# Polysketch attention then RWKV channel mix on one core: merged stores on two queues, another FFN unit order, part of the k features on GpSimd, early loads in turns, split fold

## The chip, the cores and the metric

One core of one Trainium2 chip. The metric is the device time of one execution in microseconds (us), the median of three runs; lower is better.

## What is computed

The reference, cut to what matters (B, H, S, D = 4, 4, 1088, 32; r = 8; d_model = 128; d_ff = 1024; inputs and output float32):

```python
def phi(x):                                   # r*r = 64 features per token and head
    a = einsum('rd,bhsd->bhsr', S1, x); b = einsum('rd,bhsd->bhsr', S2, x)
    return einsum('bhsi,bhsj->bhsij', a, b).reshape(..., r * r)
q_p, k_p = phi(q), phi(k)
kv = einsum('bhsf,bhsd->bhfd', k_p, v); z = sum(k_p, axis=2)
attn = einsum('bhsf,bhfd->bhsd', q_p, kv) / (einsum('bhsf,bhf->bhs', q_p, z)[..., None] + 1e-06)
x = attn as [B, S, H*D]; x_prev = x shifted by one token
xk = mu_k * x + (1 - mu_k) * x_prev;  xr = mu_r * x + (1 - mu_r) * x_prev
out = sigmoid(xr @ w_r) * (relu(xk @ w_k) ** 2 @ w_v)
```

## The kernel before

All input is loaded once, all work is on chip, and one output is stored. The program is a long list of small tasks in the string `ORDER`; each task runs on the engine named behind its slash, and every engine works through its own tasks in that order. A semaphore holds an instruction until what it reads is there, and everything behind it on that engine waits with it.

- **k side, for each batch b.** `KT` transposes k (VectorE), `KP` projects it onto S1 and S2 (TensorE, L344), `KE` copies the result out of PSUM, `KF` forms the 64 products per token and head (`outer`, L327, VectorE; the first factor is read from PSUM), `KA` accumulates them against v in PSUM (L373, L379). Then comes the fold: `KZ` masks the z part (L387), `KC` copies the kv part, `KD` does three matmuls (L398, L400), `KB` and `KW` copy the results into `kvS` and into the weights `SW` of the q side. `KC` waits for `KZ`, and `KD` for both.
- **q side, ten groups g of 128-token tiles.** `QT` transposes q, `Q1` projects (L456), `QE`, `QP`, `QD`, `QI`, `QN` make the denominator and divide, `QF` forms the products (L327), `QR` transposes them on TensorE, `QV` copies them out, `QX` multiplies by kv (L521), `XP`, `XB`, `XK`, `XL`, `XF`, `XE` build the mixed inputs.
- **FFN, ten groups of 1 to 4 tiles (`FS`).** `M1` (L562) multiplies by one 128-column unit of w_k, eight units per group; `RE` is the relu (ScalarE or VectorE), `SQ` the square of two units (mostly GpSimd, L579), `M2` (L591) the second product, `RR` and `SG` the gate, `FN` (L616) the product with the gate.
- **Stores.** `fin` stores a group straight after `FN`: for each of the four 32-row blocks of a 128-token tile one DMA, and one more where a batch ends inside the group. All go out on SyncE's queue (SP, L626), 52 in all.
- **Loads.** SP issues them in one row at the start: k0, S2, v0 in two pieces, q0, w_r, then k, v and q of the other batches. GpSimd (POOL) waits for k0 in a small copy (`gate`, L221) and then issues w_k and w_v (L222, L223), which are cast to bf16. w_k lands as `wkn`, and the task `WKP` (L281, on ScalarE) rewrites it unit by unit into `wk`, so that unit c holds the columns f with f mod 8 = c, as w_v's layout wants it.
- **Dummies.** `dummy` (L248) issues matmuls on zeros: three at the start, one more at `Z/1` in `ORDER`, between the first projection and the first `KA`.

Of the kernel before, what the change touches and what calls it, by code (L numbers as in the profile page):

```python
# [33 lines left out]
QV1_1/ACT KF1_1_0/DVE KA1_0_0/PE/b3 QX1/PE/b4 QD2/DVE KA1_1_0/PE QT1_1/DVE XP1/ACT XB1/ACT XB0/ACT XP0/ACT KZ1/DVE
QI2/DVE RR1/PE/b0 XL0/DVE KC1/ACT QT1_0/DVE XF0/POOL KD1/PE/b3 SG1/ACT XK1/DVE KT2_1/DVE RR0/PE/b0 KW1/ACT KB1/ACT
SG0/ACT Q13/PE/b4 XK0/DVE KT2_0/DVE M10_4/PE/b7 M10_2/PE/b0 M10_5/PE/b3 M10_3/PE/b1 M10_6/PE/b5 QE3/ACT M10_1/PE/b6
RE0_4/DVE RE0_2/ACT RE0_3/ACT QP3/DVE RE0_6/ACT M11_6/PE/b7 RE0_5/DVE M11_0/PE/b0 RE0_1/ACT SQ0_1/POOL M11_1/PE/b1
QD3/DVE M10_7/PE/b5 RE1_6/ACT KP2_0/PE/b3 QN2/DVE RE0_7/ACT QI3/DVE RE1_0/ACT SQ0_2/POOL QF2_1/DVE M10_0/PE/b7
M11_3/PE/b6 RE1_1/ACT KP2_1/PE/b5 RE1_3/ACT QN3/DVE SQ0_3/POOL RE0_0/ACT QF2_0/DVE M11_4/PE/b1 SQ1_0/ACT M11_7/PE/b6
M11_2/PE/b0 Q14/PE/b7 SQ0_0/POOL QF3_1/DVE RE1_4/ACT RE1_2/ACT QR2_0/PE/b1 KE2_0/ACT QT2_0/DVE SQ1_1/ACT QF3_0/DVE  # L40
M20_0/PE/b0 M20_1/PE M20_2/PE QV2_0/ACT M20_3/PE QR2_1/PE/b2 KF2_0_0/DVE RE1_7/ACT QR3_0/PE/b4 KE2_1/ACT QV2_1/ACT
QR3_1/PE/b6 FN0/DVE QV3_0/ACT KF2_1_0/DVE KA2_0_0/PE/b3 QV3_1/ACT QY2/PE/b4 M21_0/PE/b2 M21_1/PE SQ1_3/ACT M11_5/PE/b0
QX3/PE/b6 KT3_0/DVE RE1_5/ACT SQ1_2/ACT QT2_1/DVE KA2_1_0/PE XP2/ACT KT3_1/DVE M21_2/PE XL1/ACT XB2/ACT M21_3/PE
XF1/POOL KP3_0/PE/b0 XP3/ACT XK2/DVE RR2/PE/b5 FN1/DVE XB3/ACT KP3_1/PE/b1 XE0/POOL KZ2/DVE KE3_0/DVE SG2/ACT
M12_4/PE/b2 KC2/DVE M12_0/PE/b4 KE3_1/DVE M12_1/PE/b3 RE2_4/ACT M12_5/PE/b5 KF3_0_0/DVE RE2_1/ACT M12_3/PE/b2
RE2_0/ACT M12_2/PE/b3 RE2_3/DVE RE2_5/ACT M12_7/PE/b0 SQ2_0/POOL M12_6/PE/b4 RE2_2/ACT KF3_1_0/DVE RR3/PE/b2 RE2_6/ACT
KD2/PE/b5 SQ2_1/ACT KA3_0_0/PE/b4 QT3_1/DVE KA3_1_0/PE KB2/ACT KW2/ACT SQ2_2/ACT QT3_0/DVE Q15/PE/b5 XK3/DVE SG3/ACT
M22_0/PE/b1 KZ3/DVE QE5/DVE RE2_7/ACT M13_0/PE/b6 QE4/DVE M13_5/PE/b2 QP5/DVE KC3/ACT QP4/DVE M13_2/PE/b3 RE3_0/ACT
# [63 lines left out]
def kernel(  # L112
# [74 lines left out]
    for b in range(1, B):  # L187
        load_k(b, nc.sync)
        load_v(b, nc.sync)
        load_q(b, nc.sync)  # L190
# [555 lines left out]
```

## Time and profile before

| what | value |
|---|---|
| median of 3 runs | 98.9 us (98.3 to 99.4) |
| the profiled execution's own time | 98.65 us |
| its span in the profile | 96.7 us |

The span is what the profile's times count from; 1.95 us of the profiled time lie outside it. The page gives busy time by engine, the span in forty slices, the DMA queues, and the chain of work that ended last; the views of the trace give single instructions, groups of them, and stretches of time. PE is TensorE's matmuls, PEld its weight loads, DVE VectorE, ACT ScalarE, POOL GpSimd, SP SyncE; a "q" behind an engine's name means its sequencer, which issues DMAs.

### The profile page before, as it was taken

The page shows a single profiled execution, that of the slowest core. Times are in us where ns is not written, and L with a number is a line of the kernel's source. Part 1 is how long each engine was busy: PE and PEld are TensorE (multiplying, and loading weights), DVE is VectorE, ACT ScalarE, POOL GpSimd, SP SyncE. Part 2 cuts the span into 40 slices and gives each one's busy share as a digit, 9 for nine tenths or more (in the row PEclk, how much of TensorE's full clock was granted, in tenths as well). Part 3 has the DMA queues.
Part 4 walks back from the last instruction along what each step waited for, and adds up shares of the span by engine and source line. Part 5 has one row for each costly group of instructions (what it writes and reads, how often), then busy time and mean ns, then how long its engine had stood idle before and what let it go on. Part 6 is the DMA issues. An engine that isn't in the chain of part 4 may idle for free.

```text
span 96.7 us, 3021 instructions
## 1 busy us (share of the span) xinstructions
...
## 2 busy tenths in 40 slices
...
GB/s 79 236 204 258 306 286 297 293 262 350 237 209 21 26 8 27 34 0 0 7 8 101 0 7 0 40 68 53 66 0 0 41 68 63 56 0 66 88 107 41
DMA packets 9278, 9.70 MB, mean 100 GB/s; under 512 B 1456, under 2 KB 7984, under 8 KB 9264
## 3 DMA queue, kind: packets, MB, share of 16 engines
...
q0 software_dynamic: 288, 0.52, 2.9%
q8 instruction: 9, 0.15, 0.6%
q10 hardware_dynamic: 304, 0.00, 0.2%
q14 instruction: 5, 0.04, 0.1%
...
## 4 chain that ended last, share of the span: by engine, by line
PE 50%; DVE 19%; DMA 9%; ACT 5%; SPq 5%; issue 3%; ACTq 0%
PE ps_o L591 12%; PE ps_h L562 10%; DMA hdq<-in_q_dram 8%; PE ps_qtp L500 6%; PE ps_abw L456 6%; PE ps_x L521 4%; PE ps_kab L344 4%; DVE XK L534 4%; PE ps_kv L373 3%; DVE k L572 3%; DVE qp L327 3%; SPq L626 3%; PE ps_r L603 2%; DVE kT L337 1%; DMA out_dram<-osb 1%
## 5 line engine op out<-in xcount | busy, mean ns | idle before, releaser
L579 POOL TENSOR_TENSOR k<-k 128x1024 bf16<-128x1024 bf16 (+1 forms) x20 | 32.5, 1638 | 15.0 <-ACT k L570 13.0
L570 ACT ACTIVATE k<-ps_h 128x512 bf16<-128x512 f32 (+3 forms) x55 | 25.7, 540 | 1.7 <-PE ps_h L562 1.6
L562 PE MATMUL ps_h<-XK,wk 128*128 128x512 bf16 (+3 forms) x74 | 18.8, 344 | 1.0 <-DVE k L572 0.2
L591 PEld LDWEIGHTS <-k 128*128 128x128 bf16 x272 | 16.2, 98 | 4.4 <-issue 2.3
L591 PE MATMUL ps_o<-wv,k 128*128 128x128 bf16 x272 | 18.5, 219 | 0.1
L581 ACT ACTIVATE k<-k 128x1024 bf16<-128x1024 bf16 (+2 forms) x17 | 16.2, 968 | 0.1
L572 DVE TENSOR_SCALAR k<-ps_h 128x512 bf16<-128x512 f32 (+2 forms) x25 | 14.4, 622 | 0.1
L327 DVE TENSOR_TENSOR kp<-ps_kab,ab 128x512 f32<-128x512 f32 (+3 forms) x10 | 10.8, 1112 | 1.6 <-ACT ab L313 1.5
L327 DVE TENSOR_TENSOR qp<-an,ps_abw 128x512 f32<-128x512 f32 x17 | 11.2, 677 | 0.1
L456 PE MATMUL ps_abw<-SW,qT 128*128 128x96 f32 (+1 forms) x72 | 9.8, 280 | 0.6 <-DVE SW L315 0.6
L500 PE MATMUL ps_qtp<-ident,qp 128*128 128x128 f32 x68 | 9.3, 274 | 1.0 <-DVE qp L327 1.0
L562 PEld LDWEIGHTS <-wk 128*128 128x128 bf16 x80 | 7.1, 99 | 4.7 <-issue 1.3
L547 POOL TENSOR_SCALAR PP<-XL,omu_k 128x31 f32<-128x31 f32 x4 | 1.5, 381 | 18.7 <-DVE XL L315 12.5
L456 PEld LDWEIGHTS ps_abw<-SW,qT 128*128 128x128 f32 (+1 forms) x72 | 8.4, 185 | 2.1 <-DVE SW L315 0.8
L500 PEld LDWEIGHTS ps_qtp<-ident,qp 128*128 128x128 f32 x68 | 7.4, 141 | 1.9 <-PE ps_abw L456 1.1
L313 ACT COPY qpT<-ps_qtp 128x512 f32<-128x512 f32 (+1 forms) x14 | 6.7, 523 | 1.0 <-PE ps_qtp L500 0.9
L248 PE MATMUL wt<-zero 128*128 128x512 f32 x8 | 6.4, 952 | 1.1 <-DVE warm L156 1.1
L534 DVE SCALAR_TENSOR_TENSOR XK<-ps_x,mu_k,PP 128x512 bf16<-128x512 f32 (+8 forms) x13 | 6.7, 534 | 0.7 <-ACT XB L313 0.7
L344 PE MATMUL ps_kab<-SW,kT 128*64 128x64 f32 x144 | 6.0, 227 | 1.5 <-ACT qpT L313 1.3
L373 PEld LDWEIGHTS ps_kv<-kp,vt 128*32 128x32 f32 x288 | 4.5, 110 | 3.9 <-issue 1.9
L344 PEld LDWEIGHTS ps_kab<-SW,kT 128*64 128x64 f32 x144 | 4.9, 137 | 2.8 <-ACT qpT L313 1.4
L373 PE MATMUL ps_kv<-kp,vt 128*32 128x64 f32 x288 | 5.5, 221 | 1.3 <-DMA vt<-in_v_dram 0.8
...
## 6 DMA issues: line engine op xcount, KB each, us to landing
...
vt<-in_v_dram SPq DMA_DIRECT2D x4, 256.0 KB, 10.7
...
```

The lines of the kernel that those rows point to most:

```text
L327: nc.vector.tensor_mul(o.rearrange("p t h i j -> p (t h) i j"), _ap(a_, [[sa, y], [1, R], [0, R]]), _ap(b_, [[sb, y], [0, R], [1, R]]))
L344: nc.tensor.matmul(p[64 * c:64 * c + 64, (t - t0) * 64:(t - t0) * 64 + 64], kT[b][:, t, 64 * c:64 * c + 64], SW[:, 0, :H, :2, :], skip_gro ...
L373: nc.tensor.matmul(kv[32 * h:32 * h + 32, :64], vt[b][:, h, T, :], kp[:, t, h].rearrange("p i j -> p (i j)"), start=(T == 0), stop=(T == 8 ...
L456: nc.tensor.matmul(p[lo:hi, t * 96:t * 96 + 96], qT[:, s + lo:s + hi], SW[:, (s + lo) // S, g % 2:g % 2 + H].rearrange("p h x r -> p (h x ...
L500: nc.tensor.transpose(p[:, t * P:t * P + P], qp[g][:, t, 2 * pair:2 * pair + 2].rearrange("p h i j -> p (h i j)"), ident[:])
L534: nc.vector.scalar_tensor_tensor(XK[:, b * S + s:b * S + s + m], tiles[f"x_{g}"][:, c0:c0 + m], mu_k[:], PP[:, b * XW + s:b * XW + s + m], ...
L562: nc.tensor.matmul(h[:, :n * P], wk[:, c], XK[:, F0[g] * P:(F0[g] + n) * P])
L570: nc.scalar.activation(o, i, RELU)
L572: nc.vector.tensor_scalar(o, i, 0.0, None, op0=mybir.AluOpType.max)
L579: (nc.vector if eng == "DVE" else nc.gpsimd).tensor_mul(k2[:, :, :n * P], k1[:, :, :n * P], k1[:, :, :n * P])
L581: nc.scalar.activation(k2[:, :, :n * P], k1[:, :, :n * P], mybir.ActivationFunctionType.Square)
L591: nc.tensor.matmul(o[:, t * P:t * P + P], k2s[g, j][:, c, t * P:t * P + P], wv[:, w * j + c, :], start=(j == 0 and c == 0 and t == 0), sto ...
```

## The change

1. **Stores.** `FN` only computes; the stores are tasks of their own (`OD`), 36 instead of 52. Where four tiles of a group lie in one batch, the form stays (32 rows by 4 tiles by 128, four DMAs). Elsewhere one DMA stores a whole 128-token tile, its DRAM side written as 4 by 32 by 128; the tile that holds a batch's end goes in two of 2 by 32 by 128. 31 go out on SP; the last five (two of group 8, all three of group 9) on ACT.
2. **FFN unit order.** Unit c = 4x + e now holds the columns 512x + 4f + e. The weights are read in place, with a step of four elements between columns (`wkc`), `WKP` and `wkn` are gone, and w_v is loaded in the matching layout.
3. **k features on GpSimd.** The features of every batch are in two pieces per half, and nine of the sixteen run on POOL, which reads both factors from `ab` in SBUF.
4. **Early loads in turns.** q0, w_r and everything behind them are issued after small POOL copies that wait for k0, and k1 and all behind it after one that waits for v0.
5. **Split fold.** `KD` is the z matmul alone and waits for `KZ`; `KG` holds the other two and waits for `KC`; `KC` no longer waits for `KZ`.
6. **Order.** All of `ORDER` is new; `Z/1` is gone.

```diff
 ORDER = """
-Z/1 KA0_0_0/PE/b1 KA0_0_1/PE KF0_1_1/DVE KA0_1_0/PE KA0_1_1/PE QT0_0/DVE KZ0/DVE QT0_1/DVE KC0/ACT WRP/POOL KD0/PE/b1
+KD0/PE/b2 KG0/PE WRP/POOL KW0/ACT Q11/PE/b0 KB0/DVE Q10/PE/b1 QE1/DVE Q12/PE/b2 QP1/DVE QE0/DVE QD1/DVE QP0/DVE
...
-    gate = const.tile([P, 1], F32)
-    nc.gpsimd.tensor_copy(gate[:], hdk[0][:, 0, 0, :1])
-    nc.gpsimd.dma_start(wkn[:], moe_w_k)
-    nc.gpsimd.dma_start(wv[:], moe_w_v.rearrange("(p c) d -> p c d", p=P))
+    nc.gpsimd.tensor_copy(hdq[0][:, 0, :1], hdk[0][:, 0, 0, :1])
+    load_q(0, nc.sync)
+    nc.gpsimd.tensor_copy(wr_f[:, :1], hdk[0][:, 0, 0, :1])
+    nc.sync.dma_start(wr_f[:], moe_w_r)
+    nc.gpsimd.dma_start(wk[:], moe_w_k)
+    nc.gpsimd.dma_start(wv[:].rearrange("p (x e) d -> p x (e d)", e=4), moe_w_v.rearrange("(x p e) d -> p x (e d)", p=P, e=4))
+    nc.gpsimd.tensor_copy(hdk[1][:, 0, 0, :1], vt[0][:, 0, 0, :1])
+    for b in range(1, B):
+        load_k(b, nc.sync)
+        load_v(b, nc.sync)
+        load_q(b, nc.sync)
...
+        if eng == "POOL":
+            a_ = ab[:, 1, t0:t1]
+        outer(kp[:, t0:t1], a_, ab[:, 0, t0:t1], nc.gpsimd if eng == "POOL" else nc.vector)
...
+    wkc = wk[:].rearrange("p (x f e) -> p x e f", e=4, f=P)
...
-        nc.tensor.matmul(h[:, :n * P], wk[:, c], XK[:, F0[g] * P:(F0[g] + n) * P])
+        nc.tensor.matmul(h[:, :n * P], wkc[:, c // 4, c % 4], XK[:, F0[g] * P:(F0[g] + n) * P])
...
+    def stores(g):
+        n, res, t = FS[g], [], 0
+        while t < n:
+            b, x = divmod((F0[g] + t) * 4, NB)
+            m = min(n - t, (NB - x) // 4)
+            if m == 4:
+                res += [(b, x + y, m, 4, 32 * y, 32, t, m) for y in range(4)]
+            elif m:
+                res += [(b, x + 4 * i, 4, 1, 0, P, t + i, 1) for i in range(m)]
+            else:
+                res += [(b, x, 2, 1, 0, 64, t, 1), (b + 1, 0, 2, 1, 64, 64, t, 1)]
+                m = 1
+            t += m
+        return res
+    def store(g, i, eng):
+        b, x, m, step, p0, np_, t, tt = stores(g)[i]
+        o = osb[g][p0:p0 + np_, t:t + tt, :]
+        dst = orow[b][:, x:x + step * (m - 1) + 1:step, :]
+        if tt == 1:
+            o, dst = osb[g][p0:p0 + np_, t, :], dst.rearrange("a y f -> y a f")
+        (nc.scalar if eng == "ACT" else nc.sync).dma_start(dst, o)
```

SP at the end of the program before: the stores from group 6 on, all on this queue (the last 16 are groups 7, 8 and 9).

```order
L626 DMA out_dram<-osb 32x4x128 x4
L626 DMA out_dram<-osb 32x3x128
L626 DMA out_dram<-osb 32x128
L626 DMA out_dram<-osb 32x3x128
L626 DMA out_dram<-osb 32x128
L626 DMA out_dram<-osb 32x2x128 x4
L626 DMA out_dram<-osb 32x4x128 x4
L626 DMA out_dram<-osb 32x3x128 x4
```

SP at the same place now (group 6, then 7, then half of 8):

```order
L652 DMA out_dram<-osb 32x4x128 x4
L652 DMA out_dram<-osb 4x32x128
L652 DMA out_dram<-osb 2x32x128 x2
L652 DMA out_dram<-osb 4x32x128 x2
L652 DMA out_dram<-osb 32x4x128 x2
```

And ACT at the end of its program now, behind its last square and the last gate:

```order
L591 ACTIVATE k_1707<-k_1657 128x2x384
L619 ACTIVATE r<-ps_r 128x384
L652 DMA out_dram<-osb 32x4x128 x2
L652 DMA out_dram<-osb 4x32x128 x3
L770 UNCONDITIONAL_BRANCH
```

Sixteen stores stood on one queue behind `FN` of group 7; now seven stand there and five on ACT, three of them behind the last `FN`.

POOL before, from its first wait on a load to the first `XF` (names with hdk_72, vt_80, hdq_76 are k0, v0, q0):

```order
L221 COPY gate<-hdk_72 128x1
L222 DMA wkn<-in_moe_w_k_dram 128x1024
L223 DMA wv<-in_moe_w_v_dram 128x1024
L224 TENSOR_SCALAR omu_k<-mu_k 128x1
L225 TENSOR_SCALAR omu_r<-mu_r 128x1
L231 TENSOR_SCALAR wr_p<-wr_f,omu_r 128x128
L231 TENSOR_SCALAR wr_c<-wr_f,mu_r 128x128
L547 TENSOR_SCALAR PP<-XL,omu_k 128x31
```

POOL now (hdk_73 is k1):

```order
L217 COPY hdq_76<-hdk_72 128x1
L219 COPY wr_f<-hdk_72 128x1
L221 DMA wk<-in_moe_w_k_dram 128x1024
L222 DMA wv<-in_moe_w_v_dram 128x2x512
L223 COPY hdk_73<-vt_80 128x1
L229 TENSOR_SCALAR omu_k<-mu_k 128x1
L230 TENSOR_SCALAR omu_r<-mu_r 128x1
L324 TENSOR_TENSOR kp<-ab 128x512
L236 TENSOR_SCALAR wr_c<-wr_f,mu_r 128x128
L236 TENSOR_SCALAR wr_p<-wr_f,omu_r 128x128
L324 TENSOR_TENSOR kp<-ab 128x768
```

A piece of batch 0's features (kp<-ab) now stands on POOL behind the copy that waits for v0.

ACT before, from the first copy of the fold to the first copies of the q features:

```order
L313 COPY kvs<-ps_kv 128x64
L313 COPY kvS<-ps_kf 128x128
L281 COPY wk<-wkn 128x128x8
L313 COPY wsb<-ps_abw 128x128
L313 COPY qpT<-ps_qtp 128x256 x2
L313 COPY ab<-ps_kab 128x16x2x8
```

ACT now:

```order
L310 COPY kvs<-ps_kv 128x64
L310 COPY SW<-ps_kf 128x4x8
L310 COPY SW<-ps_kf 128x8
L310 COPY wsb<-ps_abw 128x128
L310 COPY ab<-ps_kab 128x16x2x8
L310 COPY qpT<-ps_qtp 128x256 x2
```

The rewriting of w_k is gone from between the fold and the copies that VectorE and TensorE wait for; `kvS` went to VectorE.

## Rows read from the trace of the kernel before

**Rows 1.** The page: its first line.

```profile
span 96.7 us, 3021 instructions
```

**Rows 2.** Busy time in two stretches: stretch, length, engines' busy us, PEclk, DMA share, GB/s.

```profile
16.00:24.00 8.00, 5.93 (x161) 4.30 (x161) 7.00 (x17) 5.77 (x14) 0.58 (x3) 1.00 1.05 307
...
26.00:88.00 62.00, 59.35 (x864) 44.48 (x869) 58.04 (x129) 55.73 (x119) 36.80 (x37) 1.00 0.18 38
```

**Rows 3.** The same view: the end of the span, and a part of it.

```profile
88.00:96.70 8.70, 0.00 (x0) 0.00 (x0) 0.19 (x1) 0.00 (x0) 0.00 (x0) 0.69 0.38 77
...
92.00:94.00 2.00, 0.00 (x0) 0.00 (x0) 0.00 (x0) 0.00 (x0) 0.00 (x0) 0.50 0.52 107
```

**Rows 4.** The output tensor, from 86.4 us to the end.

```profile
L626 SPq DMA_DIRECT2D out_dram<-osb x16: 315/425/466, 86.6 to 93.9; - x16
...
DMA to landing us min/median/max: 1.5/1.7/1.8
```

**Rows 5.** The chain that ended last, its last compute: start us, us, what.

```profile
85.72 1.88 PE ps_o L591 x32
...
87.63 0.56 DVE osb L616
```

**Rows 6.** DMA queues: packets, MB, share of 16 engines.

```profile
q0 software_dynamic: 288, 0.52, 2.9%
...
q10 hardware_dynamic: 304, 0.00, 0.2%
```

**Rows 7.** Timeline of the start: start us, us, engine, line, operation, idle before and releaser.

```profile
7.57 2.75 DVE L327 TENSOR_TENSOR kp<-ps_kab,ab 128x512 f32<-128x512 f32 x4 [1.22 <-ACT ab L313]
...
9.54 0.43 PE L373 MATMUL ps_kv<-kp,vt 128*32 128x64 f32 x16 [0.79 <-DMA vt<-in_v_dram]
...
11.32 0.21 ACT L313 COPY kvs<-ps_kv 128x64 f32<-128x64 f32 x1 [3.12 <-DVE zm L387]
...
12.95 2.02 PE L456 MATMUL ps_abw<-SW,qT 128*128 128x96 f32 x16 [0.59 <-DVE SW L315]
13.28 4.79 ACT L281 COPY wk<-wkn 128x1024 bf16<-128x1024 bf16 x1 [0.61 <-DMA wkn<-in_moe_w_k_dram]
...
15.72 1.48 DVE L337 STREAM_TRANSPOSE kT<-hdk 128x256 f32<-128x256 f32 x4
...
18.21 0.29 DVE L471 TENSOR_TENSOR pw<-ps_abw,wsb 128x128 f32<-128x128 f32 x1 [0.89 <-ACT wsb L313]
...
18.48 0.80 PE L344 MATMUL ps_kab<-SW,kT 128*64 128x64 f32 x20 [1.26 <-ACT qpT L313]
...
19.01 2.62 DVE L327 TENSOR_TENSOR kp<-ps_kab,ab 128x1024 f32<-128x1024 f32 x2
```

**Rows 8.** The chain again: q0's load, the last `XK` before the FFN, six `M1`.

```profile
3.00 7.69 DMA hdq<-in_q_dram
...
24.84 0.33 DVE XK L534
...
79.75 1.46 PE ps_h L562 x6
```

**Rows 9.** Groups on DVE, shapes apart: line, engine, operation, out<-in, count, busy us, mean ns.

```profile
L327 DVE TENSOR_TENSOR kp<-ps_kab,ab 128x1280 f32<-128x1280 f32 x3 | 4.5, 1485 | 0.3 <-ACT ab L313 0.3
...
L327 DVE TENSOR_TENSOR kp<-ps_kab,ab 128x1024 f32<-128x1024 f32 x3 | 3.7, 1221 | 0.1
...
L327 DVE TENSOR_TENSOR kp<-ps_kab,ab 128x512 f32<-128x512 f32 x3 | 2.0, 685 | 1.2 <-ACT ab L313 1.2
```

**Rows 10.** Groups on POOL, the same columns.

```profile
L579 POOL TENSOR_TENSOR k<-k 128x1024 bf16<-128x1024 bf16 x16 | 30.1, 1894 | 12.2 <-ACT k L570 10.2 <-DVE k L572 1.9
L579 POOL TENSOR_TENSOR k<-k 128x256 bf16<-128x256 bf16 x4 | 2.4, 612 | 2.8 <-ACT k L570 2.8
...
L231 POOL TENSOR_SCALAR wr_p<-wr_f,omu_r 128x128 bf16<-128x128 f32 x1 | 0.6, 610 | 3.2 <-DMA wr_f<-in_moe_w_r_dram 3.2
```

**Rows 11.** Groups on TensorE, the same columns: `M1`'s weight loads.

```profile
L562 PEld LDWEIGHTS <-wk 128*128 128x128 bf16 x80 | 7.1, 99 | 4.7 <-issue 1.3
```

More of the change, by code (lines that the diff above doesn't have):

```diff
@@ L34 @@
[L34 to L48, printed above, removed]
@@ new lines @@
+SQ0_1/ACT QF2_1/DVE M10_4/PE/b7 KA2_0_0/PE/b4 SG1/ACT SQ0_3/POOL RE0_4/ACT QD3/DVE RE1_5/ACT M20_0/PE/b3 QT2_1/DVE
+M20_1/PE RE1_2/ACT QR2_1/PE/b7 SQ0_2/POOL RE1_3/ACT KP2_1/PE/b6 QV2_1/ACT QI3/DVE SQ1_1/POOL QT2_0/DVE M20_2/PE
+M20_3/PE QN3/DVE M11_4/PE/b1 KE2_1/ACT M11_6/PE/b7 M11_0/PE/b5 FN0/DVE QR2_0/PE/b2 RE1_4/ACT QF3_1/DVE OD0_0/DMA
+KF2_1_1/POOL RE1_0/ACT M11_7/PE/b1 RE1_6/ACT Q14/PE/b3 QF3_0/DVE QV2_0/ACT RE1_7/ACT KT3_0/DVE M11_1/PE/b7
+KF2_1_0/POOL QR3_1/PE/b0 RE1_1/ACT QR3_0/PE/b1 QE4/DVE SQ1_0/ACT KT3_1/DVE KP3_0/PE/b2 QY2/PE/b7 QV3_0/ACT M21_0/PE/b5
@@ new lines @@
+QV3_1/DVE SQ1_3/POOL M21_1/PE KE3_0/ACT KA2_1_0/PE QT3_1/DVE QX3/PE/b0 SQ1_2/POOL KC2/ACT KZ2/DVE QT3_0/DVE QP4/DVE
+KD2/PE/b4 QD4/DVE KF3_0_0/POOL XP2/ACT XB2/DVE KG2/PE M21_2/PE XL1/ACT QI4/DVE M21_3/PE XB3/ACT XK2/DVE RR2/PE/b1
+XF1/POOL XP3/ACT KP3_1/PE/b6 QN4/DVE KF3_0_1/POOL FN1/DVE KW2/ACT M12_5/PE/b7 QF4_1/DVE KB2/ACT OD1_1/DMA RR3/PE/b5
+KE3_1/ACT SG2/ACT XK3/DVE Q15/PE/b4 OD1_0/DMA XE0/POOL KF3_1_0/POOL SG3/ACT QF4_0/DVE M12_1/PE/b1 RE2_5/ACT
+M13_3/PE/b0 M13_4/PE/b5 RE2_1/ACT QE5/DVE M13_1/PE/b2 KF3_1_1/DVE QR4_0/PE/b7 RE3_3/ACT M13_6/PE/b1 RE3_4/DVE
@@ L75 @@
+SQ8_2/ACT M27_3/PE RE9_0/DVE M19_1/PE/b3 M19_3/PE/b0 SQ8_3/POOL FN7/DVE M19_2/PE/b7 SQ8_1/ACT M28_0/PE/b5 RE9_2/DVE
+M19_4/PE/b6 OD7_0/DMA M19_6/PE/b4 M19_7/PE/b1 RE9_1/DVE RE9_4/ACT M19_5/PE/b2 OD7_3/DMA M28_1/PE RE9_3/DVE RE9_6/ACT
+OD7_2/DMA M28_2/PE RE9_5/ACT RE9_7/DVE OD7_1/DMA RR9/PE/b0 SQ9_1/ACT SQ9_0/DVE M28_3/PE OD7_4/DMA SQ9_3/DVE SQ9_2/ACT
+M29_0/PE/b1 FN8/DVE M29_1/PE SG9/ACT M29_2/PE OD8_3/ACT OD8_0/DMA M29_3/PE OD8_2/DMA OD8_1/ACT FN9/DVE OD9_1/ACT
+OD9_0/ACT OD9_2/ACT
 """
@@ L184 @@
     load_v(0, nc.sync)
-    load_q(0, nc.sync)
-    nc.sync.dma_start(wr_f[:], moe_w_r)
[L187 to L190, printed above, removed]
     ident = const.tile([P, P], F32)
@@ L276 @@
         add(nm, {"POOL": 0.6, "ACT": act(128, 0.105)}, lambda e, o=o, m=m: wr_mix(o, m, e), ["Lr"])
-    def wk_perm(eng):
-        o, i = wk[:].rearrange("p c f -> p f c"), wkn[:].rearrange("p (f c) -> p f c", c=NC)
-        if eng == "ACT":
-            nc.scalar.copy(o, i)
-        else:
-            nc.gpsimd.tensor_copy(o, i)
-    add("WKP", {"POOL": 2.2, "ACT": act(DFF)}, wk_perm, ["Lw"])
     QS = [2, 2, 4, 4, 4, 4, 4, 4, 4, 2]
```

125 lines of the change are left out of this document (64 added, 61 removed).

## The prediction

> **What bounds the kernel now.** I read the span first [rows 1], then busy time by stretch [rows 2, 3], then the chain of waits where compute ends [rows 5], then the output's DMAs [rows 4], and last the timeline of the start [rows 7]. Three parts show.
>
> The end: the last `FN` finishes at 87.63 + 0.56 = 88.2 us [rows 5], the span at 96.7 [rows 1]. In the 8.5 us between, every engine is empty but for that product [rows 3]. SP meanwhile issues sixteen stores one after the other, the first at 86.6 and the last at 93.9 us, so 7.3 / 15 = 0.49 us apart [rows 4]; the last lands 1.7 us after its issue, at 95.6, and 1.1 us of closing follow it. The queue's issue rate sets the end: compute has long been done.
>
> The middle: from 26 to 88 us PE is busy for 59.4 of 62 us, DVE for 58.0 and ACT for 55.7; POOL for 36.8 [rows 2]. Matmuls overlap in the pipeline, so PE's share is flattered. Nobody owns this stage: DVE and PE lead and wait for each other.
>
> The start, up to the last `XK` that the first FFN matmuls need (24.84 + 0.33 = 25.2 us [rows 8]): k features on DVE, the fold, then a DVE-heavy q stretch (7.0 of 8 us from 16 to 24 [rows 2]). ACT spends 4.79 us on rewriting w_k from 13.28, and behind it DVE waits 0.89 us for a copy and PE 1.26 us [rows 7].
>
> **The end, part by part.** FN9 still closes the compute; call its end T. Then three stores are issued by ACT, which has nothing else left. At SP's spacing of 0.49 the third is issued at T + 0.05 + 0.98. If it lands as before, 1.7 us later, and 1.1 us follow, the span ends at T + 3.8. That is the fast bound.
>
> The slow bound comes from the new form. Before, each store's outer dimension was 32 rows on both sides. Now it is 128 rows in SBUF but 4 in DRAM. The queue rows show what an outer dimension does: on q0 two weight loads of 128 rows each left 288 packets, 256 of data and 2 x 16 others; on q10 the 8-row S1 and the two 128-row mu vectors left 304 packets, 264 of data and 40 others, that is 16 + 16 + 8 [rows 6]. I read one closing packet per DMA engine in use: sixteen for 128 rows, eight for 8. Four outer rows would then mean four engines, each with 32 packets of 512 B where it had 8. From 92 to 94 us the 16 engines were 0.52 busy at 107 GB/s [rows 3]: 209 packets per us for 8.3 engine-us per us, so 40 ns each. A store's 8 packets take 0.32 us of its 1.7. Three new stores on the same four engines need 96 x 0.040 = 3.8 us behind 0.05 + 1.4, and with the 1.1 the span ends at T + 6.4.
>
> I take T + 5.1, halfway: I believe the four engines, but the 40 ns were measured with all sixteen writing, and four alone should be quicker. The tail shrinks from 8.5 to 5.1, **-3.4 us** (bounds -2.1 and -4.7). Other stores cost nothing where they stand: their queue was idle for most of the run, and the five of group 7 are issued while groups 8 and 9 are computed. The price if that cover fails is their own time on two or four engines, inside the slow bound.
>
> The Trainium skill, "DMA: Bandwidth & Descriptors", section "Why a DMA increments its semaphore by 16 and not by 1", says that a transfer runs on the largest number of engines up to 16 that divides the slowest dimension of both sides. The 8 of S1 agrees. By it the new stores use four engines, the half tiles two; the sum would then lean to the slow bound, against this change. No row here shows a four-row transfer.
>
> **The start.** *KF0 on POOL.* DVE loses one 512-column piece: its four took 2.75 us, until 10.3 [rows 7]; three end some 0.69 earlier [rows 9]. But on POOL the piece stands behind the copy that waits for v0, and v0 came at 9.54 [rows 7]. Two small instructions later, near 10.0, the piece starts. No POOL row has this shape. From 256 and 1024 columns bf16 [rows 10], (1894 - 612) / 768 = 1.67 ns a column, 0.18 fixed: 1.04 us. The only wide f32 row, 128 columns in 0.61 [rows 10], gives at most 3.3 ns, 1.9 us. I take 1.2, the same operation being the nearer row, so the piece ends at 11.2, 0.9 after the old end of the features: **+0.7**, since `KA`'s first quarter is done by then.
>
> *Split fold.* Before, from the kv copy (11.32) to the first projection (12.95) passed 1.6 us [rows 7], with mask, copy, fold, `KB` and `KW` in series. Now mask and copy go side by side and `KW` needs the first matmul alone: **-0.3**.
>
> *WKP gone.* The waits of 0.89 on DVE and 1.26 on PE go [rows 7]; they overlap, DVE is the fuller engine: **-0.9**. Late next is DVE itself.
>
> *Features of batch 1.* Of 2.62 us on DVE [rows 7] 768 columns go to POOL: **-0.9**. But `KB`, one `XP` and one `XB` move onto DVE in this stretch, and one `XL` leaves it: **+0.7**.
>
> *Loads in turns.* k0 ends as before and q0's issue slips while v0 still fills the engines, so I leave its landing at 3.00 + 7.69 = 10.7 [rows 8]: 0. `KZ` now stands on DVE behind a q0 transpose of about a microsecond, which then ends just with `KA`, near 11.7; each tenth that q0 is later shows, bounds 0 and +1. k1 now waits until v0 has landed; at some 300 GB/s [rows 2] its 0.56 MB take 1.9 us, and with issue and landing it is there at 13 to 14.5. Its transposes stood at 15.72 without a wait [rows 7] and move up to about 14.4: 0 to +0.8, I take **+0.2**. *Dummy gone:* PE was idle there in any case; PEclk was 1.00 in all compute stretches shown [rows 2]. The bounds are 0 and, if the clock fell to half for the early matmuls, some +2; I take 0.
>
> Sum -0.5; bounds -2 and +3. The FFN starts at 24.7 where it started at 25.2.
>
> **The middle.** Of the features of batches 2 and 3, 2 x (1.485 + 1.221) = 5.4 us of DVE [rows 9], all but one 512-column piece (0.69) go: -4.7. The new order gives DVE other work: two more relus, two more `QE`, `XB` and `XP` on net against ACT, which costs about half of it. Both engines together lose some 4 us, two each. POOL takes seven pieces, 4096 columns: 7 x 0.18 + 4096 x 1.67 ns = 8.1 us, at the wr_p rate 14.8; with 36.8 of 62 it has 25 free [rows 2]. PE has not a microsecond less. As it leads as often as DVE, I let 1.5 of the 2 us show: **-1.5**, bounds 0 and -4.
>
> Strided weights: no row has a step of four elements. 80 loads take 99 ns each beside matmuls [rows 11]; bounds 0, and the rival below. I take 0.
>
> **Sum.** -3.4 - 0.5 - 1.5 = -5.4: span 91.3, and with 1.95 outside it 93.25, against the profiled 98.65. That execution lies 0.25 below the median of the three runs, 98.9; I forecast **93.3**.
>
> **Rivals.**
> *A. The stores keep all sixteen engines.* For it: the same packets and bytes as before; against: the eight closing packets of the 8-row load. Tail T + 3.8: 92.0.
> *B. The middle and the start give nothing: PE holds them.* For it: PE's 59.4 of 62 us, and POOL's late first piece; against: DVE's 58.0 and the matmuls' overlap. Only the tail: 98.65 - 3.4 = 95.3.
> *C. DVE was the bound.* For it: 7.0 of 8 us before 24, 58.0 of 62 after; against: ACT close behind, and PE. Then 4.0 of the 4.7 us show: 93.3 - 2.5 = 90.8.
> *D. Slower: the strided w_k.* A step of four elements reads 8 bytes for 2. If that stretches a load fourfold, 80 loads of 396 ns stand where 99 did. Six `M1` in a row take 1.46 us [rows 8], 0.24 each, so about 0.15 us per load shows: 80 x 0.15 = +12, 105.3. It decides when a load shows by 5.4 / 80 = 68 ns, that is from about 0.31 us on. Against: today's 99 ns hide behind 0.24.
> The Trainium skill, "TensorE: Matmul & The Clock Gate", sections "LDWEIGHTS" and "Weight-path perf modes", lets a load's time follow its column count, and allows steps up to 1,024 elements for the fast load; by this rule D costs nothing. Only contiguous loads are in this trace.
>
> **How the numbers follow.** Forecast 0.47, A 0.2, B 0.18, C 0.11, D 0.04. The range, 90.6 to 95.8, runs from C to B with B's half microsecond of spread; outside it are D, the slow side of B and the fast side of C, under 0.2. About 1% is what a measurement of this kernel can tell from no change: faster 0.94 (all but D and the far side of B), same 0.02, slower 0.04.
>
> **What would show it.** Right: the last compute near 86 us, three ACT issues behind it, 5 us to the span's end; landing of the new stores well over 1.7 us; the last `XK` before the first FFN matmuls near 24.7; no ACT wait of DVE near 18; L562's successor still loading in about 99 ns; POOL near 48 us busy. Wrong: landing at 1.7 (A); compute still ending at 88 (B) or before 84 (C); weight loads far over 99 ns (D); a PEclk under 1.00 before 24 us.

## The result, and the profile after

The changed kernel takes 95.43 us, median of 4 runs (94.91 to 97.02), against 98.9 us: ratio 0.963, 95% interval 0.955 to 0.971. The forecast was 93.3 with 90.6 to 95.8. A ratio here compares the runs near each kernel's fastest, so it can lie below the ratio of the medians; medians and spread are given beside it.

The profiled run took 94.91 us. Its windows (stretch, then busy us of PE, PEld, DVE, ACT and POOL, PEclk, DMA share, GB/s), which answer to [rows 2, 3]:

```profile
8.00:16.00 8.00, 5.65 (x109) 4.99 (x110) 4.88 (x16) 0.66 (x4) 2.71 (x6) 0.73 1.10 262
16.00:24.00 8.00, 7.08 (x133) 5.58 (x136) 7.15 (x21) 2.69 (x8) 1.51 (x1) 0.63 1.05 298
26.00:88.00 62.00, 59.41 (x868) 46.68 (x874) 56.58 (x133) 54.80 (x119) 45.30 (x45) 1.00 0.19 45
88.00:92.90 4.90, 0.00 (x0) 0.00 (x0) 0.00 (x0) 0.00 (x0) 0.00 (x0) 0.72 0.26 75
```

ACT's w_k copy is gone, POOL has 8.5 us more in the middle, and the granted clock, 1.00 from 16 to 24 us before, is 0.63 there and 0.73 in the eight us ahead.

The timeline of its start (start us, us, engine, line, operation, idle before and releaser), which answers to [rows 7]:

```profile
8.35 0.18 POOL L223 COPY hdk<-vt 128x1 f32<-128x1 f32 x1 [2.13 <-DMA vt<-in_v_dram]
8.36 0.43 PE L372 MATMUL ps_kv<-kp,vt 128*32 128x64 f32 x16 [0.67 <-DVE kp L324]
...
8.81 1.06 POOL L324 TENSOR_TENSOR kp<-ab 128x512 f32<-128x512 f32 x1
...
9.93 0.47 PE L372 MATMUL ps_kv<-kp,vt 128*32 128x64 f32 x18 [1.09 <-POOL kp L324]
...
11.12 0.21 ACT L310 COPY kvs<-ps_kv 128x64 f32<-128x64 f32 x1 [2.93 <-PE ps_kv L378]
11.37 0.19 DVE L386 TENSOR_TENSOR zm<-ps_kv,mask 128x32 f32<-128x32 f32 x1 [0.54 <-ACT kvs L310]
...
11.61 0.64 PE L396 MATMUL ps_kf<-zm,S 128*128 128x32 f32 x2 [0.55 <-DVE zm L386]
12.18 0.70 PE L402 MATMUL ps_kf<-ident,kvs 128*64 128x128 f32 x4
12.92 0.25 ACT L310 COPY SW<-ps_kf 128x32 f32<-128x32 f32 x2 [1.59 <-PE ps_kf L402]
...
13.23 3.73 PE L463 MATMUL ps_abw<-SW,qT 128*128 128x96 f32 x16 [0.35 <-ACT SW L310]
...
25.73 0.80 DVE L541 SCALAR_TENSOR_TENSOR XK<-ps_x,mu_k,PP 128x256 bf16<-128x256 f32 x2
```

The sixteen matmuls of q's first projection, 2.02 us before [rows 7], take 3.73; they start 0.28 later than before. The last `XK` ends at 25.73 + 0.80 = 26.53, where it ended at 25.17 [rows 8].

How long this start takes varies with the loads. Two kernels of the tail experiments below have the same program up to here; their last `XK` ends at 27.82 (first line) and 25.63 (second line), after waits for q0 of 1.77 and 0.43 us where the changed kernel's profile has none. In both the granted clock falls as well, to 0.55 and 0.70 from 16 to 24 us.

```profile
27.02 0.80 DVE L541 SCALAR_TENSOR_TENSOR XK<-ps_x,mu_k,PP 128x256 bf16<-128x256 f32 x2
```

```profile
24.83 0.80 DVE L541 SCALAR_TENSOR_TENSOR XK<-ps_x,mu_k,PP 128x256 bf16<-128x256 f32 x2
```

DVE's last three `FN`, the output's DMAs from 83 us (duration ns min/median/max, first and last start us), a window of the tail, and the queues; they answer to [rows 3 to 6]:

```profile
82.31 0.69 DVE L628 TENSOR_TENSOR osb<-ps_o,r 128x512 f32<-128x512 f32 x1 [0.25 <-issue]
85.71 0.69 DVE L628 TENSOR_TENSOR osb<-ps_o,r 128x512 f32<-128x512 f32 x1
87.06 0.56 DVE L628 TENSOR_TENSOR osb<-ps_o,r 128x384 f32<-128x384 f32 x1 [0.66 <-ACT r L619]
...
L652 SPq DMA_DIRECT2D out_dram<-osb x7: 323/542/560, 83.0 to 86.8; - x7
L652 ACTq DMA_DIRECT2D out_dram<-osb x5: 385/547/653, 86.4 to 88.9; - x5
...
90.00:92.00 2.00, 0.00 (x0) 0.00 (x0) 0.00 (x0) 0.00 (x0) 0.00 (x0) 0.54 0.20 60
...
q1 hardware_dynamic: 7484, 8.65, 35.6%
q0 software_dynamic: 416, 0.52, 3.2%
q10 hardware_dynamic: 988, 0.33, 1.4%
```

The last `FN` ends at 87.62, the span at 92.9. So the three parts come to: start +1.36 (25.17 to 26.53), middle -1.93 (63.02 to 61.09 us), tail -3.23 (8.51 to 5.28). Forecast: -0.5, -1.5, -3.4.

### The profile page after: what moved, and what is told of

It is laid out like the page before. It is cut to its first block, busy times and chain, and to the rows that moved or that the text cites. A ratio compares the mean times of both kernels' runs of the same rounds, so it can differ in the third digit from the quotient of the medians.

```text
span 92.9 us, 3009 instructions
## 1 busy us (share of the span) xinstructions
PE 80.3 (86%) x1197; PEld 61.9 (67%) x1203; DVE 73.8 (80%) x186; ACT 63.0 (68%) x145; POOL 54.0 (58%) x75
## 4 chain that ended last, share of the span: by engine, by line
PE 43%; ACT 28%; DVE 8%; DMA 6%; issue 5%; POOL 2%; SPq 2%; DVEq 0%; ACTq 0%; POOLq 0%
ACT k L580 12%; PE ps_abw L463 8%; ACT k L591 7%; PE ps_qtp L507 7%; PE ps_h L572 6%; DMA vt<-in_v_dram 6%; PE ps_kv L372 6%; PE ps_kab L341 4%; PE ps_o L601 3%; PE ps_x L528 3%; ACT qpT L310 3%; ACT r L619 2%; DVE kT L334 2%; PE ps_kf L402 2%; ACT PP L537 2%
## 5 line engine op out<-in xcount | busy, mean ns | idle before, releaser
L589 POOL TENSOR_TENSOR k<-k 128x1024 bf16<-128x1024 bf16 (+2 forms) x21 | 33.1, 1588 | 9.9 <-ACT k L580 7.6
L582 DVE TENSOR_SCALAR k<-ps_h 128x512 bf16<-128x512 f32 (+2 forms) x27 | 15.9, 628 | 1.7 <-PE ps_h L572 1.7
L591 ACT ACTIVATE k<-k 128x1024 bf16<-128x1024 bf16 (+3 forms) x17 | 16.8, 1027 | 0.1
L324 POOL TENSOR_TENSOR kp<-ab 128x512 f32<-128x512 f32 (+1 forms) x9 | 10.9, 1216 | 10.2 <-ACT ab L310 9.6
L463 PE MATMUL ps_abw<-SW,qT 128*128 128x96 f32 (+1 forms) x72 | 11.4, 309 | 0.5 <-ACT SW L310 0.5
L463 PEld LDWEIGHTS ps_abw<-SW,qT 128*128 128x128 f32 (+1 forms) x72 | 10.3, 216 | 1.8 <-ACT SW L310 1.1
L572 PEld LDWEIGHTS <-wk 128*128 128x128 bf16 x80 | 8.0, 115 | 4.0 <-DVE XK L541 0.8
L310 ACT COPY qpT<-ps_qtp 128x512 f32<-128x512 f32 (+1 forms) x15 | 8.0, 545 | 2.5 <-PE ps_qtp L507 2.3
L628 DVE TENSOR_TENSOR osb<-ps_o,r 128x512 f32<-128x512 f32 (+3 forms) x10 | 6.1, 607 | 1.7 <-ACT r L619 0.7
L324 DVE TENSOR_TENSOR kp<-ps_kab,ab 128x512 f32<-128x512 f32 (+1 forms) x7 | 4.9, 726 | 1.8 <-ACT ab L310 1.8
```

The lines of the kernel that those rows point to most:

```text
L310: nc.scalar.copy(o, i)
L324: eng.tensor_mul(o.rearrange("p t h i j -> p (t h) i j"), _ap(a_, [[sa, y], [1, R], [0, R]]), _ap(b_, [[sb, y], [0, R], [1, R]]))
L463: nc.tensor.matmul(p[lo:hi, t * 96:t * 96 + 96], qT[:, s + lo:s + hi], SW[:, (s + lo) // S, g % 2:g % 2 + H].rearrange("p h x r -> p (h x ...
L572: nc.tensor.matmul(h[:, :n * P], wkc[:, c // 4, c % 4], XK[:, F0[g] * P:(F0[g] + n) * P])
L582: nc.vector.tensor_scalar(o, i, 0.0, None, op0=mybir.AluOpType.max)
L589: (nc.vector if eng == "DVE" else nc.gpsimd).tensor_mul(k2[:, :, :n * P], k1[:, :, :n * P], k1[:, :, :n * P])
```

## The experiments

Three questions: why the start became longer, what made the tail shorter, and what gave the middle. Ratios are to the kernel before, run beside each. In the edits to `ORDER`, only the stretch of a line that changed is shown.

### The start: fillers and the GpSimd piece

**The filler put back** (`Z`: two matmuls of 512 columns whose result nobody reads):

```diff
-KA0_0_0/PE/b2 KF0_1_0/DVE
+Z/1 KA0_0_0/PE/b2 KF0_1_0/DVE
```

> The changed kernel with the one block of filler matmuls put back on TensorE between the first projection and the first state matmuls, as the kernel before had it. Theory 1 (clock): without the filler TensorE stood empty from 7.7 to 8.4 us and from 8.8 to 9.9, and its granted clock fell to half from 11.6 to 21.9 us; that is what made the start 1.35 us longer instead of 0.5 shorter. Then PEclk reads 1.00 from 8 to 24 us, the 16 matmuls of the first projection of q (L463) go from 3.73 back to about 2.0 us, the last XK ends near 25.2 instead of 26.5, and the time falls by 1.0 to 1.6 us, to about 94.1. Theory 1b: the clock matters, but the wait for the GpSimd piece (1.09 us) is still there, and one filler is not enough: the fall comes later or is shorter. Theory 2 (rival): the start is held by the GpSimd piece and by the work moved onto VectorE, and a slower TensorE is hidden: the last XK stays at 26.5 +- 0.3 and the time at 95.4 +- 0.4, whatever the clock.

Median 95.88 us, ratio 0.951 (0.946 to 0.957); of the six runs two took 94.2 us, at a mean clock of 0.966, and four 95.6 to 96.6, at 0.93. The profiled run is one of the two. Its clock is 1.00 to 16 us and falls after that; its last `XK` ends at 25.59:

```profile
16.00:24.00 8.00, 6.52 (x158) 5.10 (x158) 6.91 (x20) 3.16 (x10) 2.06 (x4) 0.79 1.06 254
```

In this profile it is theory 1b: the fall comes later and is shorter. By the median (95.88 against 95.43) one filler alone gains nothing.

**Three fillers**:

```diff
-KF0_1_1/DVE KA0_0_1/PE KA0_1_0/PE QT0_1/DVE KA0_1_1/PE
+KF0_1_1/DVE Z/1 KA0_0_1/PE KA0_1_0/PE QT0_1/DVE KA0_1_1/PE Z/1
```

(and the one above).

> The changed kernel with three blocks of filler matmuls: the one of before, one while TensorE waits for the GpSimd piece, one between the state matmuls and the fold. Theory 1: the clock stays at 1.00 to 24 us and the last XK ends at 25.2 or earlier, time 93.8 to 94.4; if one filler is enough, no better than with one, and the third may cost up to 0.5 us where it stands in front of the fold (the wait there was 0.55 us, a block of two matmuls takes about 1.1 us at the full clock where nothing overlaps). Theory 2: 95.4 +- 0.4 or later.

93.98 us, ratio 0.949 (0.945 to 0.952), 1.45 below the changed kernel; five of the six runs lie from 93.65 to 94.13, one at 98.19. Two windows of it, and three rows of its timeline:

```profile
8.00:16.00 8.00, 7.34 (x122) 4.68 (x121) 5.67 (x18) 1.04 (x5) 2.71 (x6) 1.00 1.12 261
16.00:24.00 8.00, 6.49 (x172) 5.00 (x172) 8.00 (x23) 3.50 (x11) 2.34 (x5) 1.00 1.05 297
...
9.21 1.12 PE L253 MATMUL wt<-zero 128*128 128x512 f32 x2
...
13.32 2.02 PE L463 MATMUL ps_abw<-SW,qT 128*128 128x96 f32 x16 [0.35 <-ACT SW L310]
...
23.64 0.80 DVE L541 SCALAR_TENSOR_TENSOR XK<-ps_x,mu_k,PP 128x256 bf16<-128x256 f32 x2
```

The granted clock is 1.00 in both stretches, the projection is back at 2.02 us, and the last `XK` ends at 24.44, 2.1 us earlier. VectorE, which waited for TensorE in the changed kernel (7.15 of 8 us busy from 16 to 24), is now busy for all 8.00. Theory 2 falls for the changed kernel: VectorE doesn't cover a TensorE at half clock. A part is given back: last `XK` to last `FN` is 62.0 us here, 61.1 in the changed kernel.

**The kernel before without its filler**:

```diff
-Z/1 KA0_0_0/PE/b1 KA0_0_1/PE
+KA0_0_0/PE/b1 KA0_0_1/PE
```

> The kernel before without its block of filler matmuls (it computes nothing that is used); nothing else is changed. Theory 1: the loss belongs to the filler alone: the granted clock falls to half at some 11 to 12 us for about ten us, the first projection of q takes about 3.7 instead of 2.02 us, and the time rises by 1 to 2 us, 98.9 to about 100.3. Theory 1b: the filler is not enough by itself, the GpSimd wait of the changed kernel is needed too: the clock stays at 1.00 and the time at 98.9 +- 0.4. Theory 2: the clock may fall, but VectorE covers it: time 98.9 +- 0.5.

99.08 us, ratio 0.999 (0.995 to 1.004). The clock dips late, and nothing follows:

```profile
16.00:24.00 8.00, 6.98 (x160) 5.40 (x160) 6.97 (x17) 5.23 (x14) 0.35 (x2) 0.79 1.06 308
```

Theory 1 in its first form falls: the filler alone was worth nothing to the kernel before. There the dip stayed without effect on the time, as theory 2 had it.

**The first GpSimd piece back on VectorE**, no fillers:

```diff
-KF0_0_1/POOL
+KF0_0_1/DVE
```

> The changed kernel with the one piece of batch 0's k features that went to GpSimd put back on VectorE; the fillers stay out, the later pieces stay on GpSimd. Theory 1b (the clock falls because filler and GpSimd wait come together): without the GpSimd wait TensorE is idle no longer than in the kernel before without its filler, so the clock falls briefly or not at all (0.79 or more in 16 to 24 us), the last XK ends near 25.2, time 94.2 to 94.9. Theory 1 in its first form (the filler alone): the clock falls as in the changed kernel and the time stays at 95.4. Rival of both: the piece costs VectorE its 0.69 us and the start gets longer: last XK at 26.5 or later, time 95.4 to 96.1.

Median 94.67 us, ratio 0.937 (0.930 to 0.944); three runs took 92.7 to 94.0 us (mean clock 0.982 to 0.996) and five 94.6 to 96.1 (0.929 to 0.967). In the profiled run, of 94.0 us, the clock is 1.00 up to 24 us and the last `XK` ends at 25.27:

```profile
16.00:24.00 8.00, 5.36 (x160) 3.97 (x156) 7.07 (x20) 3.13 (x10) 2.21 (x4) 1.00 1.05 304
```

The rival that VectorE would miss the relief falls. Taken with the others: in the profiled runs the GpSimd piece alone (one filler put back) or the missing filler alone (here, and in the kernel before) leaves the clock at 1.00 up to 16 us and at 0.79 or more from there to 24. With both, TensorE sat idle 0.67, 1.09 and 0.55 us between 7.7 and 11.6 us, and then its clock fell (the timeline of the changed kernel above).

### The tail: form, queues, order

**The last group's stores over 32 rows**, on both queues:

```diff
-            if m == 4:
+            if m >= 3:
...
-FN9/DVE OD9_1/ACT
-OD9_0/ACT OD9_2/ACT
+FN9/DVE OD9_1/DMA
+OD9_0/ACT OD9_2/ACT OD9_3/DMA
```

> The changed kernel with the last group's three stores (each of 4 rows in DRAM by 128 partitions) replaced by four stores of 32 partitions with three rows each, two on each queue; nothing else is changed. Theory 1 (four engines): the three stores ran on four DMA engines, 44 closing packets = 2 x 16 + 3 x 4; with 32 outer rows each is spread over 16 engines: 4 x 16 closing packets instead of 3 x 4, so queue q10 changes by +52 when two of the four run on it and the rest of the closing packets show on q1; the stretch from the last FN to the span's end shrinks from 5.25 to about 0.05 + 0.5 + 1.7 + 1.1 = 3.4 us, time 95.4 to about 93.6. Theory 2 (rival): the tail is issue, a fixed landing time and closing: four stores on two queues take as long as three on two, 5.25 us, or 0.2 more; time 95.4 +- 0.4.

93.68 us (92.23 to 94.79), ratio 0.939 (0.933 to 0.944). Its queues:

```profile
q1 hardware_dynamic: 7708, 8.75, 36.8%
q0 software_dynamic: 416, 0.52, 3.4%
q10 hardware_dynamic: 816, 0.23, 1.1%
```

The last `FN` ends at 88.98 in this profile, the span at 92.8: tail 3.8 instead of 5.3, as theory 1 had it (3.4). The packet counts that the expectation sketched were wrong, the rule behind them holds. In the changed kernel q10 carried 304 packets of the loads and ScalarE's five stores: 640 of data, and 988 - 304 - 640 = 44 others, 2 x 16 + 3 x 4. Here its four stores leave 816 - 304 - 256 - 192 = 64, 4 x 16. Compute ended 1.4 us later than in the changed kernel's profile, and 1.3 of that was there at the last `XK`, where VectorE had waited 1.8 us for q0. The stores cannot reach back there; the median shows the gain.

**The kernel before with the new stores alone**: `stores` and `store` of the changed kernel called in its `fin`, group 9's three on ScalarE's queue, group 8's on both.

```diff
-        for y in range(4):
...
-                nc.sync.dma_start(orow[b][:, x:x + 4 * m - 3:4, :], o[32 * y:32 * y + 32, t:t + m, :])
+        for i in {8: (3, 0, 2, 1), 9: (1, 0, 2)}.get(g, range(len(stores(g)))):
+            store(g, i, "ACT" if g == 9 or (g, i) in ((8, 3), (8, 1)) else "SP")
```

> The kernel before with the new store form alone (same groups, group 9's three on ScalarE's queue, group 8's on both); nothing else of the change. Theory 1: the tail shrinks from 8.5 to 5.25 us and nothing else moves: time 98.99 - 3.25 = 95.7, the same as the whole change gives. Rival: the stores in the middle take part (fewer, or on few engines beside the loads): time under 95.2 or over 96.3 with the last FN moved from 88.2.

99.87 us, ratio 1.009 (1.005 to 1.013): slower by a little. Theory 1 is refuted. First the last three `FN` of the kernel before, then this kernel's, with its stores:

```profile
85.85 0.68 DVE L616 TENSOR_TENSOR osb<-ps_o,r 128x512 f32<-128x512 f32 x1
...
86.94 1.25 DVE L616 TENSOR_TENSOR osb<-ps_o,r 128x512 f32<-128x512 f32 x2
```

```profile
85.84 0.69 DVE L618 TENSOR_TENSOR osb<-ps_o,r 128x512 f32<-128x512 f32 x1
...
86.56 5.58 SPq L644 DMA_DIRECT2D out_dram<-osb  x7
86.94 1.24 DVE L618 TENSOR_TENSOR osb<-ps_o,r 128x512 f32<-128x512 f32 x2
...
L644 SPq DMA_DIRECT2D out_dram<-osb x7: 322/536/559, 86.6 to 91.8; - x7
...
SPq L644 <- DMA out_dram<-osb: 1.9, 1, 1.9
```

The `FN` haven't moved, and the tail is 97.5 - 88.2 = 9.3 us where it was 8.5. Twelve stores stand where sixteen stood, but SP needs 5.58 us for its seven. An issue takes 0.54 us in the median, and ahead of the last one SP waited 1.9 us for an earlier store to land (the last line: us in total, times, longest). Eight of the twelve have four outer rows or two, and by the packet counts above these go to as few engines. They land late. By the semaphores in the trace, group 9's three, issued by ScalarE from 89.1 to 91.0 us, land at 94.4, 95.4 and 96.4, behind group 7's five, of which the last lands at 93.8. In the changed kernel, where group 7's five are issued 3.5 us earlier, the same three land at 90.3, 91.05 and 91.8, each 2.6 to 2.9 us after its issue. That the eight share the same engines is argued from these times and from the packets; no run tried it alone.

**The changed kernel with the old stores**: its order, all stores in 32-row form on SP's queue.

```diff
+                nc.sync.dma_start(orow[b][:, x:x + 4 * m - 3:4, :], o[32 * y:32 * y + 32, t:t + m, :])
...
     def store(g, i, eng):
+        return
```

> The changed kernel, its order unchanged, with the stores of the kernel before: 32 rows each, all on SP's queue, none on ScalarE's. The new stores alone brought nothing to the kernel before (99.87), where the last three FN end within 1.7 us (86.5, 87.6, 88.2); in the changed kernel they end at 83.0, 86.4 and 87.6. Theory A (the order makes the tail): eight stores of group 7 from 83.05 at 0.49 each, four of group 8 and four of group 9 behind them, the last issued near 90.4; with 1.7 to land and 1.1 to close the span ends at 93.2, 5.6 us after the last FN, time 95.4 to 95.9. Theory B (form and second queue make it): the tail is 8 us or more as before, time 98 or more.

Median 96.5 us, ratio 0.968 (0.964 to 0.973), against 0.963 (0.955 to 0.971) for the change as it is. Its last two `FN` and its stores from 80 us:

```profile
85.57 0.68 DVE L628 TENSOR_TENSOR osb<-ps_o,r 128x512 f32<-128x512 f32 x1
86.92 0.56 DVE L628 TENSOR_TENSOR osb<-ps_o,r 128x384 f32<-128x384 f32 x1 [0.67 <-PE ps_o L601]
...
L639 SPq DMA_DIRECT2D out_dram<-osb x16: 315/426/451, 82.9 to 90.2; - x16
```

Sixteen stores on one queue, 0.49 us apart as before, and the tail is 93.0 - 87.48 = 5.5 us. Theory A holds: the order makes the tail. It brings `FN7` out 4.6 us before the last `FN` instead of 1.7, so that group 7's eight stores have been issued when groups 8 and 9 come. Form and second queue together add 0.2 us to that in the profiles; the medians lie 1.1 us apart (96.5 and 95.43) and the intervals of the ratios overlap, so what they add is not settled.

### The middle, and the strided weights

**All eight later GpSimd pieces on VectorE** (on the kernel with three fillers):

```diff
-KF1_1_0/POOL
+KF1_1_0/DVE
...
-KF3_1_0/POOL
+KF3_1_0/DVE
```

> The changed kernel with the three fillers (93.98 us, clock at 1.00), and with all eight pieces of batches 1 to 3 that stood on GpSimd put on VectorE, at the same places of the order. What it tells is where the middle's gain comes from (last XK to last FN, 61.1 us in the changed kernel against 63.0 before). Theory A: VectorE's relief is worth it: the pieces add some 8 x 0.6 to 0.7 = 5.4 us to VectorE, and half to all of it shows: time 96 to 99. Theory B: TensorE leads, or the order alone gives the gain: time 94 to 95.

97.16 us, ratio 0.980 (0.975 to 0.985), 3.2 us over the kernel with fillers: theory A. VectorE's busy time grows from 73.5 to 78.6 us; 3.2 of these 5.1 us show. They don't all show in the middle. A window of this profile, its last `XK` and its last `FN`:

```profile
26.00:28.00 2.00, 2.00 (x15) 1.75 (x15) 1.82 (x5) 0.94 (x6) 0.14 (x1) 0.50 1.04 257
...
25.52 0.43 DVE L541 SCALAR_TENSOR_TENSOR XK<-ps_x,mu_k,PP 128x224 bf16<-128x224 f32 x1
...
89.28 0.56 DVE L628 TENSOR_TENSOR osb<-ps_o,r 128x384 f32<-128x384 f32 x1 [0.67 <-ACT r L619]
```

The last `XK` ends at 25.95 where the kernel with fillers has 24.44: two of the eight pieces stand on VectorE ahead of it. From there to the last `FN` 63.9 us pass, against 62.0. So 1.5 us show before the middle and 1.9 in it, and as the clock fell to 0.50 in this profile, a part of the 1.9 may be the clock's. Without the GpSimd pieces the new order would have lost the middle's gain (63.0 before, 62.0 with fillers).

**w_k read contiguously**, on the same kernel; the hidden units no longer match w_v's rows:

```diff
-    wkc = wk[:].rearrange("p (x f e) -> p x e f", e=4, f=P)
+    wkc = wk[:].rearrange("p (x e f) -> p x e f", e=4, f=P)
```

> The changed kernel with the three fillers (93.98 us), and with the slices of w_k read contiguously, so that the hidden units stand in another order than w_v's rows expect (the output is therefore not the reference's). Rival D of the prediction, in its mild form, is what is tested: a load with a step of four elements took 115 ns in the changed kernel, against 99 before. If the loads hide behind the matmuls, as the prediction took it: loads back at 99 ns, time unchanged, 93.98 +- 0.4. If each load shows: 80 x 16 ns = 1.3 us less, 92.7.

94.0 us, ratio 0.951 (0.949 to 0.953): no gain. The loads of the changed kernel, then of this one (count, busy us, mean ns):

```profile
L572 PEld LDWEIGHTS <-wk 128*128 128x128 bf16 x80 | 8.0, 115 | 4.0 <-DVE XK L541 0.8 <-issue 0.4 <-ACT k L580 0.2
```

```profile
L572 PEld LDWEIGHTS <-wk 128*128 128x128 bf16 x80 | 7.1, 100 | 4.2 <-DVE XK L541 0.8 <-issue 0.4 <-ACT k L580 0.3
```

The step of four elements costs a load 15 ns, and the matmuls hide it.

### The repairs together

**Fillers and 32-row stores** (the second and the fifth edit above in one kernel):

> The changed kernel with both repairs: the three blocks of filler matmuls and the last group's stores over 32 rows. If the two gains are independent: last FN near 86.4 us as with the fillers alone, tail 3.8 us as with the 32-row stores alone (3.82 measured), span 90.3, time about 92.4, some 1.5 below the fillers alone (93.98). Rival: the two meet (an earlier end of compute finds the queue of the other groups' stores still busy): tail 4.5 or more, time 93.1 or more.

93.27 us, ratio 0.940 (0.935 to 0.946). The tail is 3.7 us (87.89 to 91.6), so the stores' gain stands, but in the profile the last `XK` ended 0.9 us and the last `FN` 1.4 us later than with the fillers alone, and the clock is 0.50 from 27 to 29 us. VectorE had waited 1.26 us for q0 and later 0.71 us for batch 2's k. The two gains didn't add up, and for another reason than the rival's: by this profile the loads came later.

**First piece on VectorE, a filler before the state matmuls and one before the fold, 32-row stores**:

> Three repairs of the changed kernel together: the first piece of k features on VectorE, one block of fillers before the first state matmuls and one before the fold, the last group's stores over 32 rows on two queues. If the gains add up: last XK near 24.9, last FN near 86.0, tail 3.8, span 89.8, time 91.8 with little scatter. Rival: the fillers are not needed with the piece on VectorE, or the earlier start is given back in the middle: last FN at 86.6 or later, time 92.5 or more.

92.65 us, ratio 0.934 (0.929 to 0.939); four runs from 91.5 to 92.75, two of 94.9 and 95.3. The profiled run is one of those two, and its chain of waits and VectorE's timeline say why:

```profile
8.82 8.49 DMA hdk<-in_k_dram
...
17.41 1.49 DVE L334 STREAM_TRANSPOSE kT<-hdk 128x256 f32<-128x256 f32 x4 [1.73 <-DMA hdk<-in_k_dram]
```

Batch 1's k took 8.49 us from issue to landing.

**The same without the copy that holds k1 back**:

```diff
-    nc.gpsimd.tensor_copy(hdk[1][:, 0, 0, :1], vt[0][:, 0, 0, :1])
```

> The three repairs together (92.65 us, single runs from 91.5 to 95.3), and without the one copy that holds batch 1's k back until v0 has landed; the other two copies (before q0 and before the load of w_r) stay. The scatter of the versions with loads in turns is wider than that of the kernel before (97.9 to 99.4 in most runs); in the profiled run of the three repairs k1 took 8.49 us from issue to landing (8.82 to 17.32), VectorE waited 1.73 us for it and the last XK ended at 28.0 instead of 24.4. Theory A (the gate brings k1 late, and by how much is luck): without it the spread of the runs is under 1.5 us, k1's transposes wait for nothing, and the median falls to 91.0 to 91.9. Theory B (the gate is worth its price): k1 now shares the engines with v0, v0 lands 0.8 to 1.2 us later than 8.5, the state matmuls start at 9.4 or later, and the median is 92.6 to 93.6.

92.24 us (91.39 to 94.18), ratio 0.927 (0.921 to 0.934); the interval overlaps the last one. Of theory A, k1's transposes wait for nothing and the last `XK` ends at 24.6, but the spread stays at 2.8 us. Theory B's late v0 doesn't show: the first state matmuls start at 9.35, but right behind a filler (8.29 + 1.13 = 9.42), and wait for no load. What holding k1 back is worth is not settled. By its median this is the fastest kernel of the study, some 3.7% below the changed one (0.927 / 0.963).

## Why the prediction was right, and where not

The time came within the range and the direction was right. The forecast was 2.1 us low; in the profiled run it is 1.7, the start 1.9 longer than forecast, the tail 0.2 longer, the middle 0.4 shorter. In number the result is rival B's (95.3), but not by B's mechanism: the middle did gain, and the start lost most of it.

**The start, -0.5 forecast, +1.36 measured.** The step that failed is "*Dummy gone:* ... The bounds are 0 and, if the clock fell to half for the early matmuls, some +2; I take 0". The upper bound was near the truth, and the prediction's own sign of being wrong, a PEclk under 1.00 before 24 us, came. The reason given, that the clock was 1.00 in all compute stretches shown, was a fact of a kernel that had the filler and no GpSimd wait; it couldn't speak for one without the filler and with the wait. The size of this term is uncertain by about a microsecond: with the same start, other profiles end the last `XK` at 25.63 and 27.82. With three fillers the last `XK` ends at 24.44, 2.1 us earlier and 0.3 from the forecast 24.7. The other terms can be read there at full clock: the first projection starts 0.37 later than before (forecast +0.7 - 0.3), with a filler ahead of the fold, and from there to the last `XK` 1.1 us are gained (forecast -0.9 - 0.9 + 0.7 + 0.2 = -0.9).

The first two terms were wrong and partly cancel. v0 had landed by 8.35, not 9.54; which of the loads now held back had been in its way, no run shows by itself. The GpSimd piece took 1.06 us, as the same operation on bf16 would have it (1.04): it ended at 9.87 instead of 11.2, and the state matmuls ended 0.1 us later than before (11.06 against 10.93), not 0.7. But from there to the projection 2.17 us pass in the changed kernel and 2.02 did before: the split fold's -0.3 doesn't show. Its premise failed in the trace. Mask and copy don't go side by side: the mask starts at 11.37, after the copy has ended at 11.33, and the profile names the copy as what VectorE waited for. Nor does `KW` go ahead on the first matmul alone: it starts at 12.92, when the fold's other matmuls (12.18 + 0.70) are done. The half clock lengthens the fold's matmuls as well, so how much the split could give is open.

**The tail, -3.4 forecast, -3.23 measured.** The size was right, four engines too: the 44 closing packets show them. The time of a packet was the guess; from 90 to 92 us 0.20 of 16 engines move 60 GB/s, 117 packets per us, so 27 ns each, and the slow bound with 27 in place of 40 gives 0.05 + 1.4 + 96 x 0.027 + 1.1 = 5.1. The Trainium skill's rule in "DMA: Bandwidth & Descriptors", "Why a DMA increments its semaphore by 16 and not by 1" (as many engines, up to 16, as divide the slowest dimension on both sides), is borne out by both counts, 3 x 4 and 4 x 16. The new stores landed well over 1.7 us after their issue (2.6 to 2.9), as the prediction's sign had it. The credit was wrong: the prediction followed the last three stores and named group 7's in a half-sentence. In the profiles the old stores in the new order lose only 0.2 us, and the new ones in the old order lose 0.8. So that the -3.4 came out as a gain of the new stores is in part luck: their tail was priced rightly, but most of the difference was the order's. Rival A was half right: sixteen engines give the shorter tail, and the changed kernel doesn't have them.

**The middle, -1.5 forecast, -1.93 measured.** Moving the eight pieces to GpSimd is worth 3.2 us in all, 63% of VectorE's relief, and at most 1.9 of it lies in the middle. That fits the prediction's view that VectorE holds as much as TensorE; the mechanisms of rival C (all of it shows) and B (nothing) both fall. At full clock the earlier start gives some of the middle back: 62.0 us, so -1.0.

**Strided weights, 0 forecast.** Right: 115 ns in place of 99, hidden. Rival D falls. The Trainium skill, "TensorE: Matmul & The Clock Gate", "LDWEIGHTS", lets the time follow the columns alone; here the step adds 15 ns, and the measurement decides.
